# A convolution ahead of a two-layer network: columns 16 to 31 added on VectorE, and the softmax sums of batches 3 to 15 made by accumulating transfers

## The chip, the cores and the metric

The kernel runs on one core of a Trainium2 chip. The metric is the device time of one execution in microseconds (us); before the change the median of three runs is 410.81 us. Below, PE is TensorE, DVE is VectorE, ACT is ScalarE, POOL is GpSimd and SP is SyncE.

## The reference

```
w = exp(weight_gen - max); w = w / sum(w)        # softmax over the K = 7 taps, per position and head
out[b, s, h, g] = sum_k w[b, s, h, k] * x_pad[b, s + k, h, g]      # 8 heads, 192 channels
h1 = out @ w1;  h2 = out @ w2                    # 192 -> 1024
result = maximum(h1, h2) @ w_out                 # 1024 -> 192
```

x is 8 x 4160 x 192, in float32. The 33,280 positions lie on 128 partitions with 260 positions, here called columns, on each.

## The kernel before, in words

**Batches, units, tiles.** The 260 columns are cut into 17 batches: batches 0 to 15 of 16 columns and batch 16 of 4. A batch is cut into units: of 4 columns in batches 0 and 1 (units 0 to 7), of 8 after that. A unit has as many tiles as columns, so tile t has its number in common with a column; a tile holds one eighth (in a 4-column unit, two eighths) of the 1024 hidden values of its unit's columns. Tiles go through PE in groups, of two up to tile 15 and of three from tile 16 (GROUPS, L71).

**Softmax.** For batch b, `load_wg` (L101) brings the taps in, `exp_sum` (L131, ACT) writes their exponentials to `e_t`, `red` (L143, DVE) adds the seven of each head, `ln` (L149, ACT) takes the logarithm of the sums, `shift` (L153, DVE) subtracts it from the taps, and `weights` (L159, ACT) takes the exponential again, which is the normalised weight, written twice in bf16.

**Convolution.** `mul` (L173, DVE) multiplies the seven shifted copies of x by the weights into `m_t`. `adds` (L188, DVE) sums the seven taps in three instructions: taps 3 to 5 onto 0 to 2 (L198), two pairs (L204), and the last pair into `y_t` (L207). Its argument `beside` puts other small DVE steps between the three: a third of `shift` of the next batch, or a half of `red` of a later one. `transpose` (L212) moves `y_t` of a unit through a transposing transfer issued by SP into `yt`. On POOL it then queues a one-element copy (`gate`, L224) that waits for that `yt`, and behind it the loads of x for a later batch and of the taps of batch b + 3.

**The first columns take another way.** `sum_transpose` (L239) sums and transposes on PE: for each of 6 slices and for each tap it multiplies a part of `m_t` by the identity, accumulating in PSUM, and ACT copies the result to `yt` (L255). Units 0 to 4 sum all seven taps so; units 5 to 7 only taps 0, 1, 2 and 6 (`LEFT`), after DVE has done the first of its three additions (`adds(..., first=True)`).

**The two layers.** `hid_tile` (L291, PE) makes a tile's difference of the two products and `relu` (L306, ACT) its positive part; `out_first` and `out_second` (L345, L361, PE) multiply that by w_out (L339) and add the unit's columns times `w10`, the product of w1 and w_out (L351), which gives the results of finished columns, and `evac` (L377, ACT) copies them out of PSUM. `hidden` (L458) puts one group in order: the tiles but one, the first half of the results, relu, the last tile, the second half, the copy out. The results that a group takes (`OUTS`, L426 to L432) are planned from when units are complete, with at most 2 or 4 columns in a group.

**What sets the order.** The order on each engine is the order in which the program writes its instructions; nothing is moved by a scheduler. From group 8 on, `steps` (L768) writes the ACT steps of the softmax at fixed tile numbers (`due`, L721 to L732) and the DVE steps in `extra` (L748): `mul` of the next batch at tile 0 of a batch, its second half at tile 8, and so on. The groups before that have hand-written steps (`early`, L712). Waits are made from the reads and writes of the tiles. POOL issues in order: an instruction that waits holds all behind it.

## Time and profile before

| what | value |
|---|---|
| median of three runs | 410.81 us (410.8 to 415.66) |
| the profiled execution, first to last instruction | 409.1 us |
| PE matmul busy | 398.8 us (97%), 7350 instructions |
| DVE busy | 374.4 us (92%), 219 instructions |
| ACT busy | 357.4 us (87%) |
| POOL busy | 68.7 us (17%) |
| transfers issued by SP, share of the 16 engines | 36.0% |
| transfers issued by POOL, share of the 16 engines | 29.5% |
| granted TensorE clock, mean | 0.997 |

The span is 1.7 us below the median of the runs, which also hold what lies before the first and after the last instruction. Busy shares are means over the whole span; whether an engine's time sets the end must be read from the waits. A busy PE here is nearly one without gaps: matmuls follow each other, and the "idle before" columns name the gaps.

### The profile page before, as it was taken

To read this page: it belongs to the slowest core of one execution; us is meant where nothing else is said; L and a number is where in the kernel's file an instruction comes from. 1 tells how busy PE (TensorE), PEld (TensorE's weight loads), DVE (VectorE), ACT (ScalarE), POOL (GpSimd) and SP (SyncE) were. 2 spreads that over 40 slices of the span, in tenths; PEclk is the share of its full clock that TensorE was granted. 3 is DMA by queue.
4 is the path that set the end of the run, shared out by engine and by line. 5 is a ranking of instruction groups with operands and counts; after the bars stand their busy time and mean duration, and the time that the engine had idled before them with its cause. 6 is when DMAs were issued, how large, how long until landed. Compare 5 with 4: busy or idle time off the path is not lost.

```text
span 409.1 us, 15992 instructions
## 1 busy us (share of the span) xinstructions
PE 398.8 (97%) x7350; PEld 317.1 (78%) x7350; DVE 374.4 (92%) x219; ACT 357.4 (87%) x424; POOL 68.7 (17%) x101
## 2 busy tenths in 40 slices
PE   7999999999999999999999999999999999999995
PEld 2688999677777777777777777777787777787795
DVE  6999999999999999999999999999999999999000
ACT  6899989999999988999988999988999989888771
POOL 0321101222211021221101221210122212210000
PEclk9999999999999999999999999999999999999998
DMA  8966667658657874963796497489648648744513
GB/s 245 250 152 164 116 151 186 143 143 184 150 97 219 217 118 99 260 176 74 224 195 146 96 251 180 82 195 238 120 106 241 166 64 244 151 89 79 213 61 136
DMA packets 60384, 65.68 MB, mean 161 GB/s; under 512 B 47615, under 2 KB 48511, under 8 KB 60318
## 3 DMA queue, kind: packets, MB, share of 16 engines
q1 hardware_dynamic: 51934, 40.54, 36.0%
q0 software_dynamic: 8240, 24.04, 29.5%
q8 instruction: 57, 0.93, 0.9%
q10 hardware_dynamic: 144, 0.10, 0.1%
q14 instruction: 9, 0.07, 0.1%
HBM read 35.96 MB, written 25.56 MB: 150 GB/s over the span
## 4 chain that ended last, share of the span: by engine, by line
DVE 73%; PE 17%; issue 4%; DMA 4%; SPq 0%; DVEq 0%; ACT 0%
DVE m_t L182 37%; DVE m_t L198 15%; DVE m_t L204 10%; PE op_ps L339 9%; PE hd L299 7%; DVE sum_t L147 3%; DVE y_t L207 3%; DVE wg_t L156 3%; DMA xs<-in_x_dram 3%; PE op_ps L351 2%; DMA yt<-y_t 1%; DVE wd L582 0%; DVE xb_t L618 0%; SPq L521 0%; SPq L104 0%
## 5 line engine op out<-in xcount | busy, mean ns | idle before, releaser
L309 ACT ACTIVATE rd_t<-hd 128x1024 bf16<-128x1024 f32 (+1 forms) x206 | 234.6, 1189 | 28.0 <-PE hd L299 26.5
L339 PE MATMUL op_ps<-wo,rd_t 64*128 64x192 bf16 x4160 | 210.6, 243 | 0.1
L339 PEld LDWEIGHTS <-rd_t 64*128 64x128 bf16 x4160 | 180.8, 94 | 15.7 <-ACTq L372 0.3
L299 PE MATMUL hd<-yt,wd 64*128 64x512 bf16 (+1 forms) x1584 | 187.3, 360 | 1.4 <-ACT rd_t L309 1.2
L182 DVE TENSOR_TENSOR m_t<-xb_t,en_t 128x10752 bf16<-128x10752 bf16 (+1 forms) x37 | 187.4, 5071 | 0.2
L299 PEld LDWEIGHTS <-wd 64*128 64x128 bf16 x1776 | 94.1, 94 | 43.3 <-issue 3.3
L224 POOL CAST gate<-yt 128x1 f32<-128x1 bf16 x29 | 34.0, 1171 | 275.7 <-DMA yt<-y_t 275.7
L198 DVE TENSOR_TENSOR m_t<-m_t 128x4608 bf16<-128x4608 bf16 (+1 forms) x32 | 76.8, 2401 | 0.1
L395 ACT COPY o_t<-op_ps 128x384 f32<-128x384 f32 (+1 forms) x99 | 57.3, 591 | 13.4 <-PE op_ps L339 13.3
L351 PE MATMUL op_ps<-w,yt 64*128 64x192 bf16 x780 | 55.5, 243 | 1.1 <-ACT o_t L395 1.0
L351 PEld LDWEIGHTS <-yt 64*128 64x128 bf16 x780 | 38.4, 94 | 17.5 <-issue 2.1
L204 DVE TENSOR_TENSOR m_t<-m_t 128x3072 bf16<-128x3072 bf16 (+1 forms) x29 | 50.0, 1724 | 0.1
L167 ACT ACTIVATE en_t<-wg_t 128x896 bf16<-128x896 f32 (+2 forms) x45 | 35.3, 820 | 0.0
L207 DVE TENSOR_TENSOR y_t<-m_t 128x1536 bf16<-128x1536 bf16 (+1 forms) x29 | 27.3, 941 | 0.5
L385 DVE COPY o_last<-op_ps 128x192 f32<-128x192 f32 x1 | 0.4, 358 | 25.9 <-ACT o_last L385 25.9
L156 DVE TENSOR_TENSOR wg_t<-wg_t,sum_t 128x280 f32<-128x280 f32 (+5 forms) x46 | 22.0, 481 | 0.0
L147 DVE TENSOR_REDUCE sum_t<-e_t 128x64 f32<-128x448 f32 (+2 forms) x31 | 19.6, 636 | 2.6 <-ACT e_t L135 2.6
L114 POOL DMA_DIRECT2D xb_t<-in_x_dram x33 | 17.7, 535 | 23.3 <-ACT rd_t L309 11.8
L135 ACT ACTIVATE e_t<-wg_t 128x896 f32<-128x896 f32 (+2 forms) x18 | 16.1, 899 | 2.5 <-DMA wg_t<-in_weight_gen_dram 2.5
L309 ACT ACTIVATE rd_t<-hdp 128x1024 bf16<-128x1024 f32 x16 | 16.2, 1048 | 0.6 <-PE hdp L299 0.6
L613 PE MATMUL warm<-ident 128*128 128x512 bf16 x38 | 11.0, 457 | 2.6 <-DVE ident L560 2.6
L299 PE MATMUL hdp<-yt,wd 64*128 64x256 bf16 x192 | 12.9, 269 | 0.1
(46 smaller groups left out, 73.6 us busy)
## 6 DMA issues: line engine op xcount, KB each, us to landing
out_dram<-o_t SPq DMA_DIRECT2D x28, 768.0 KB, 5.0
xb_t<-in_x_dram POOLq DMA_DIRECT2D x30, 384.0 KB, 5.2
wg_t<-in_weight_gen_dram POOLq DMA_DIRECT2D x14, 448.0 KB, 5.2
xb_t<-xb_t POOLq DMA_DIRECT2D x16, 288.0 KB, 5.2
out_dram<-o_t SPq DMA_DIRECT2D x8, 384.0 KB, 2.9
wg_t<-in_weight_gen_dram SPq DMA_DIRECT2D x2, 448.0 KB, 4.5
xs<-in_x_dram SPq DMA_DIRECT2D x2, 384.0 KB, 6.0
xb_t<-in_x_dram POOLq DMA_DIRECT2D x3, 192.0 KB, 5.1
```

The source lines that it names most:

```text
L156: nc.vector.tensor_tensor(out=w_t, in0=w_t, in1=_sub(s_ts[b], hs.start, [[1, hs.stop - hs.start], [0, K]]), op=ALU.subtract)
L167: nc.scalar.activation(out=_sub(en_ts[b], (o * WGC + j * N * K) * 2, [[2 * N, K], [2, N], [1, 2]]), in_=_sub(wg_ts[b], (o * H + j * N) * K ...
L182: return nc.vector.tensor_tensor(out=m_out, in0=x_in, in1=_sub(en_ts[b], o * WGC * 2, [[2, K * n * H], [0, G // 2], [1, 2]]), op=ALU.mult,)
L198: nc.vector.tensor_tensor(out=taps(0, 1, 3), in0=taps(0, 1, 3), in1=taps(3, 1, 3), op=ALU.add)
L204: nc.vector.tensor_tensor(out=taps(0, 2, 2), in0=taps(0, 2, 2), in1=taps(1, 5, 2), op=ALU.add)
L207: nc.vector.tensor_tensor(out=_sub(y_ts[b], o * D, [[64, 2], [P, 3 * w // 2], [1, 64]]), in0=taps(0, 1, 1), in1=taps(2, 1, 1), op=ALU.add,)
L224: nc.gpsimd.tensor_copy(out=gate, in_=yt[:, 0:1])
L299: nc.tensor.matmul(hid_out(t, f, j), lhsT=wd_at(j, s, f // 4, f % 4 * P, P), rhs=_sub(yt_ts[u][half(j), :], (s + j) % 3 * P, [[3 * P, w // ...
L309: relu_of[t0] = nc.scalar.activation(out=rd[:, k * 1024:(k + n) * 1024], in_=hd[:, at:at + n * 1024], func=AF.Relu)
L339: return nc.tensor.matmul(op_out(c), lhsT=rd[half(r), k * 1024 + at:k * 1024 + at + P], rhs=wo[half(r), f * D:(f + 1) * D], start=False, s ...
L351: nc.tensor.matmul(op_out(c + j), lhsT=yt_ts[u][half(j), (3 * i + (s + j) % 3) * P:(3 * i + (s + j) % 3 + 1) * P], rhs=w10[half(j), s * D: ...
L395: nc.scalar.copy(out=_sub(o, c % 24 * D, [[D, len(qs)], [h * D, 2], [1, D]]), in_=_sub(tile_, at + (qs[0] - p) * D, [[D, len(qs)], [512, 2 ...
```

## The change

Batch 1 is cut into two units of 8 columns, and is summed by DVE and moved by transposing transfers like the later batches; only batch 0 keeps 4-column units and `sum_transpose`. So `adds` runs in full for both units of batch 1, the steps for units 4 to 7 on PE and their ACT copies are gone, and with `ready` computed from the larger units the plan of results changes in the first groups: group 4 takes no results where it took 2 columns.

For batches 3 to 15 (`by_dma`), `exp_sum` writes `e_t` as seven planes, one for each tap, and `tap_planes` adds them by three accumulating transfers issued by POOL, each reading what the one before it wrote: planes 3 to 5 onto 0 to 2, then planes 2 and 6 onto 0 and 1, then plane 1 onto 0. `red` does nothing for these batches and `ln` reads plane 0. Their `shift` is done in six parts, three beside each `adds`, where it was in three beside the first. The tile numbers of the ACT steps are new, and the taps are loaded half a batch earlier.

```
-        for w in (4, 4, 4, 4) if b < 2 else (8, 8) if n == 16 else (n,):
+        for w in (4, 4, 4, 4) if b == 0 else (8, 8) if n == 16 else (n,):
...
     def exp_sum(b, i=0, of=1):
...
+        if by_dma(b):
+            N = BATCHES[b][1] * H
+            nc.scalar.activation(out=_sub(e_ts[b], 0, [[N, K], [1, N]]), in_=_sub(wg_ts[b], 0, [[1, K], [K, N]]),
+                                 func=AF.Exp)
+            return
...
+    def by_dma(b):
+
+        return 3 <= b < NB - 1
+
+    def tap_planes(b):
+
+        N, e_t = BATCHES[b][1] * H, e_ts[b]
+        for to, frm in (((0, [[1, 3 * N]]), (3 * N, [[1, 3 * N]])),
+                        ((0, [[N, 2], [1, N]]), (2 * N, [[4 * N, 2], [1, N]])),
+                        ((0, [[1, N]]), (N, [[1, N]]))):
+            nc.gpsimd.dma_start(out=_sub(e_t, *to), in_=_sub(e_t, *frm), accum_op=ALU.add)
...
     def ln(b, i=0, of=1):
+        if by_dma(b):
+            N = BATCHES[b][1] * H
+            s_ts[b] = psm.tile([P, N], FP32, name="sum_t", tag="sum")
+            nc.scalar.activation(out=s_ts[b], in_=e_ts[b][:, 0:N], func=AF.Ln)
+            return
...
     def transpose(u):
...
-        if o == 0 and b + 3 < NB:
-            load_wg(b + 3, nc.gpsimd)
+        if u == 4:
+            load_wg(4, nc.gpsimd)
+        if o == 8 and b + 4 < NB:
+            load_wg(b + 4, nc.gpsimd)
...
-        weights(1, 4)
-        mul(1, 4)
         relu(rd, 7, 1)
         exp_sum(2)
-        red(2)
-        adds(1, 4, True)
+        adds(1, 0, beside=lambda i, of: red(2, i, 2) if i < 2 else None)
         sum_transpose(3)
         weights(1, 8)
...
     def end_of_1():
-        shift(2)
-        adds(1, 8, True)
-        mul(1, 12)
+        transpose(4)
         exp_sum(3)
-        red(3)
-        adds(1, 12, True)
+        tap_planes(3)
+        adds(1, 8, beside=lambda i, of: shift(2, i, 2) if i < 2 else None)
...
     early = {
-        3: (none, rest_of_1),
-        4: (lambda: (behind(relu_of[8], load_x(2, 0, 8, halo=False)), sum_transpose(4),
-                     behind(yt_of[4], load_wg(4, nc.gpsimd))), end_of_1),
-        5: (lambda: sum_transpose(5, LEFT), none),
-        6: (lambda: (behind(relu_of[12], load_x(2, 8, 8)), weights(2, 8), ln(3), sum_transpose(6, LEFT)), none),
-        7: (lambda: (behind(relu_of[14], load_x(3, 0, 8)), sum_transpose(7, LEFT)), none),
+        4: (lambda: behind(relu_of[8], load_x(2, 0, 8, halo=False)), lambda: ln(2), end_of_1),
     }
 
     due = {}
-    for c in range(3, NB):
-        soon = c < 8
-        parts_ = [(16 * (c - 2) + (8 if soon else 10 if c < NB - 1 else 15), True, lambda c=c: weights(c, 0))]
-        if 8 in dict(pieces(c)):
-            parts_.append((16 * (c - 2) + (14 if soon else 15), True, lambda c=c: weights(c, 8)))
+    for c in range(2, NB):
+        t0 = 16 * (c - 2)
+        if c == 2:
+            parts_ = [(16, True, lambda: weights(2, 0)), (20, True, lambda: weights(2, 8))]
+        else:
+            parts_ = [(t0 + (11 if c < NB - 1 else 15), True, lambda c=c: weights(c, 0)),
+                      (t0 + 3, False, lambda c=c: ln(c))]
+            if 8 in dict(pieces(c)):
+                parts_.append((t0 + 20, True, lambda c=c: weights(c, 8)))
         if c > 3:
-            ln_at = -2 if c == 4 else 0 if c < 8 else 2 if c < 11 else 4
-            parts_.append((16 * (c - 2) + ln_at, False, lambda c=c: ln(c)))
-            parts_.append((16 * (c - 3) + (4 if c < 8 else 7), True, lambda c=c: exp_sum(c)))
+            parts_.append((t0 - 14, True, lambda c=c: (exp_sum(c), by_dma(c) and tap_planes(c))))
...
-        if s == 8 + later and b + 2 < NB:
-            adds(b + 1, 8, beside=lambda i, of: red(b + 3, i, 2) if b + 3 < NB and i < 2 else None)
-        if k == n // 4 - 1 and 7 < u + 1 < NU:
+        if s == 13 and b + 2 < NB:
+            adds(b + 1, 8, beside=lambda i, of: (shifts(b + 2, 3 + i) if by_dma(b + 2) else None,
+                                                 red(b + 3, i, 2) if b + 3 < NB and i < 2 else None))
+        if k == n // 4 - 1 and u + 1 < NU:
             transpose(u + 1)
+
+    def shifts(c, i):
+
+        if c < NB:
+            shift(c, i, 6 if by_dma(c) else 3)
```

## The prediction

> **What bounds the kernel now.** I read the chain of waits first. It names DVE.
>
> ```profile
> DVE 73%; PE 17%; issue 4%; DMA 4%; SPq 0%; DVEq 0%; ACT 0%
> DVE m_t L182 37%; DVE m_t L198 15%; DVE m_t L204 10%; PE op_ps L339 9%; PE hd L299 7%; DVE sum_t L147 3%; DVE y_t L207 3%; DVE wg_t L156 3%; DMA xs<-in_x_dram 3%; PE op_ps L351 2%; DMA yt<-y_t 1%; DVE wd L582 0%; DVE xb_t L618 0%; SPq L521 0%; SPq L104 0%
> ```
>
> DVE carries it until 328 us, then PE to the end. But a chain follows whatever came last, by however little. So next the timeline where it changes engine (start, duration, engine, line; in brackets the idle time before, and who ended it):
>
> ```profile
> 327.12 0.96 DVE L207 TENSOR_TENSOR y_t<-m_t 128x1536 bf16<-128x1536 bf16 x1
> ...
> 328.23 1.42 SPq L216 DMA_TRANSPOSE yt<-y_t  x1
> ...
> 333.50 0.82 PE L299 MATMUL hd<-yt,wd 64*128 64x512 bf16 x6 [0.20 <-DMA yt<-y_t]
> ...
> 333.58 0.21 POOL L224 CAST gate<-yt 128x1 f32<-128x1 bf16 x1 [10.63 <-DMA yt<-y_t]
> ```
>
> PE waited 0.20 us for this `yt`, its only wait on a transposed unit. Elsewhere the gate copy on POOL marks the landing: unit 8 (tiles from 32) at 61.68, while PE reaches tile 32 at 68.93 (in its timeline 18 matmuls start at 68.27, 12 of them tile 31). The lead is 7.3 us there, 3.9 at tile 96 (155.6 against 159.5), 1.2 at tile 200, 0 at tile 216, and after that about 1 again, as the last batches need fewer small steps. DVE needs 23.67 us per batch (`mul` at 67.66 to `mul` at 91.33), PE 23.09 (tile 72 at 124.95 to tile 208 at 321.21, 8.5 batches). DVE loses to PE slowly and ends level. Both bound the kernel; PE has nearly no gaps, as its busy time by stage shows (from:to, length, then busy us and instructions of PE, PEld, DVE, ACT, POOL):
>
> ```profile
> 30.00:59.60 29.60, 28.60 (x768) 27.93 (x770) 29.60 (x17) 27.95 (x39) 3.22 (x6) 1.00 0.66 148
> 59.60:113.00 53.40, 52.51 (x925) 42.00 (x921) 53.33 (x31) 49.00 (x57) 12.17 (x15) 1.00 0.69 162
> 113.00:333.00 220.00, 219.60 (x3813) 171.09 (x3810) 219.66 (x120) 199.56 (x224) 39.74 (x54) 1.00 0.69 164
> ```
>
> From 113 to 333 PE idles 0.4 us of 220, at full clock. So taking work off DVE brings nothing by itself. What counts is when PE gets going and what it has left.
>
> **PE's own work.** Units 4 to 7 had 84 + 3 x 48 matmuls of `sum_transpose`: 1.23 us at 34.13 and 0.70 each at 38.24, 42.78 and 46.36, 3.3 us in all. The hidden tiles cost the same (a 4-column tile, 12 matmuls, 0.66 us; an 8-column tile, 6 matmuls, 0.66 us). So PE's floor is 409.1 - 3.3 = 405.8, or 407.5 with the 1.7 us around the span. By that alone the kernel can't gain 2%.
>
> **DVE.** Away go 26 reductions: 24 of 64 sums at 0.614 and batch 3's 1.08, 15.8 us. `adds` of batch 1 takes 2 x (2.55 + 1.75 + 0.955) = 10.5 in place of 3 x 1.35: +6.4. `shift` in six parts: rows of 128x112 at 0.269 and 128x280 at 0.443 give 0.327 for 168; so 2 x 0.269 + 4 x 0.327 = 1.85 for 1.39, 0.46 busy, of which 0.08 per extra instruction overlaps its neighbour: +0.23 on the path per batch. Per batch DVE then needs 23.67 - 2 x 0.53 + 0.23 = 22.84, under PE's 23.09. The loss of lead ends.
>
> **The first 60 us, step by step.** DVE reaches `mul(2,0)` later: full `adds` (+6.2 with overlaps), one `mul` less to start (-0.3), no `red(3)` (-1.0), the sums and shift of batch 2 in halves (+0.2): 44.0 becomes about 49.3. On the way `y_t` of unit 4 ends at 37.5; the first transfer took 5.7 from there (55.9 to 61.68), so `yt` lands at 43.2, just when PE wants tile 16 (43.5, below). The second ends at 49.4.
>
> Group 4 gives PE no results now. Counting `OUTS` by its formula, 16 columns have results when tile 25 starts, where 20 had; the four are made good only by group 18. Two columns cost 0.25 + 1.32 = 1.57 us (6 matmuls of L351, 32 of L339), so PE carries 3.1 us of its work past tile 25.
>
> ACT: relu 9 ends at 34.0, `ln(2)` waits for the sums on DVE until 35.0, then `exp_sum(3)` (0.9) and relus of 0.95 follow: relu 15 ends at 43.4, so PE starts tile 16 at 43.5 (47.43 before). Relus 16 to 18 and the copy end at 48.3, `weights(2,0)` at 49.3, `exp_sum(4)` at 50.8 (its taps land about 49.9), relus 19 to 21 and the copy at 54.0. Then comes `ln(3)`. PE, with hidden PSUM for three tiles, idles meanwhile: tile 19 waits until 47.0, tile 22 until 52.7.
>
> **The sums by transfers.** `tap_planes(3)` is three transfers, each issued after the landing of the one before, all on POOL. POOL's queue ahead of them: the gate for unit 4 (43.3, up to 1.8 us long in the rows), a load of x, a load of taps (0.53 and 0.55); so the first goes out at about 45.0. Behind POOL's waits stand `tap_planes(4)`, the gate of unit 5 and the x of batch 3, due for `mul(3,0)` at 74 and here by 68: covered by 6 us.
>
> No row shows an accumulating transfer. The nearest is the copy within SBUF, `xb_t<-xb_t`, 288 KB: alone in the queue at 30.06 it landed in 2.5 us; the median, queued behind a load of x, is 5.2:
>
> ```profile
> xb_t<-xb_t POOLq DMA_DIRECT2D x16, 288.0 KB, 5.2
> ```
>
> is the page's row of the whole span (number of issues, size, median from issue to landing), and from 28 to 34 us the only one is
>
> ```profile
> xb_t<-xb_t POOLq DMA_DIRECT2D x1, 288.0 KB, 2.5
> ```
>
> The first link stands behind two loads: 5.2, landing at 50.3. The others stand alone and are smaller, but read their destination too: between 2.5 and 5.2, I take 3.0 each. A link below 2.5 isn't excluded for 64 and 128 KB; at 1.8 the wait is gone. Sum: 50.3 + 6.0 = 56.3, against ACT's arrival at 54.0. ACT stands 2.4 us with relu 22 behind `ln(3)`; PE waits for that relu, and DVE with `shift(3)`, done with `mul(2,0)` at 55.1, waits too. Then `ln` 0.3, `weights(2,8)` 1.05, relus 22 and 23 1.9: PE starts tile 25 at 59.7. Before it was 59.6.
>
> The Trainium skill's page "DMA: Bandwidth & Descriptors", section "Rules for kernel authors", speaks against this tree of sums: a transfer that reads what another wrote must wait for that one's completion. Its section "Anatomy of one DMA — SWDGE (gpsimd) path" fits a fixed 2.0 us plus bytes at 436 GB/s, an estimate of 2.3 and 2.2 for the last two links; by it the sums would be there at 54.8 and the span 1.5 us shorter. For the 288 KB of the lone copy the fit gives 2.7 where the trace has 2.5; for an accumulating one no row here shows it.
>
> **The sum.** Before, PE went from tile 25 at 59.6 to the end at 409.1. Now: 59.7 + 349.5 + 3.1 = 412.3, less the 0.2 waited at 333.5: 412.1. Later starvation I cost at nothing, since the units lead: `adds(2,0)` runs from 56.8 to 62.6 and its `yt` lands at 66.6, PE takes tile 32 at 69.0; tile 40's lands at 78.0, wanted at 81.4; and then DVE is the faster. If that cover were gone, the late transfers (5.4 against a median of 3.9) would cost up to 1.5. Later sums have room: from `exp_sum(c)` to `ln(c)` are 17 tiles, 24.5 us, against 5.2 + 6.0; for batches 5, 8, 11 and 14, whose transfers are written after a gate, some 3 us remain at links of 4.5. ACT loses four copies of 0.82, under cover. With 1.7 around the span: **414 us**, 0.7% slower, within 2%.
>
> **The rivals.** First, no wait at `ln(3)`: links of 1.8, or the first not behind the loads (45.0 + 3 x 2.5 = 52.5). Then relu 22 starts 2.4 earlier: 409.7, 411.4 with the rest; were the other early gaps (tiles 19 and 22) smaller too, down to the floor of 407.5. For it: the transfers are small. Against: POOL's queue holds two loads just ahead.
>
> Second, slower: the links cost 5.2 and more. At 5.2 `ln(3)` runs at 60.7, and the time is 418.2; from 5.7 on it is over 419.0, the 2% bound. At 7.0 it is 422, and the transfers of batches 5, 8, 11 and 14, which start only behind a gate, come 2 us late four times: 430. For it: 15 of the 16 copies in the trace took over 4 us, the transfer engines are 69% busy, and two of the three move runs of 512 bytes, where the copy moves 2304. Against: those copies stood behind a load.
>
> Third, faster by over 2%: the chain is to be taken at its word and DVE sets the end. Then the 11 batches of sums before 328 us are worth 11 x 1.06 - 11 x 0.23 - 5.3 = 3.8 us: 407. Even that isn't 2%; it needs a PE gap that no view shows.
>
> **How the numbers follow.** `ln(3)` holds ACT by a few us: 0.52, 411 to 418. No wait: 0.24. Slow links: 0.20. Faster by over 2%: 0.04 (2% is about what a measurement here tells from no change). So within 2% has 0.76. The range runs from 407, the floor, to 423, links of about 7 without the repeats.
>
> **What would show it.** ACT's wait on a transfer of `e_t` at `ln` of batch 3, near 54 us, and no other; tile 25 near 59.7 us, and a lead of the units over PE that stays at 2 to 4 us afterwards; PE without gaps from 60 us on; no reductions after batch 3. I am wrong if PE idles after 113 us, if tile 25 starts after 62, or if a link is over 5.7 us.

## The result, and the profile after

The changed kernel takes 461.36 us, median of 4 runs (453.76 to 471.82), against 411.36 before (four runs, one more than in the table above): ratio 1.1062, 95% interval 1.0944 to 1.1179. It is 11% slower, where the prediction had 414 us. The profiled execution took 464.18 us with a span of 462.3; it is one of the two longer ones, and the ratio is formed from the other two (453.76 and 458.53).

The page's chain of work that ended last, by engine and by line, no longer reads like two engines without gaps:

```profile
PE 36%; DMA 20%; issue 19%; DVE 9%; POOL 9%; ACT 5%; POOLq 0%; ACTq 0%; SPq 0%; DVEq 0%
PE op_ps L361 15%; PE hd L321 14%; DMA e_t<-e_t 11%; DMA xb_t<-in_x_dram 6%; DVE m_t L206 5%; POOL e_t L152 3%; POOL gate L246 3%; ACT rd_t L331 3%; DMA yt<-y_t 3%; PE op_ps L373 3%; PE warm L635 2%; DVE m_t L222 2%; DMA xb_t<-xb_t 1%; DVE m_t L226 1%; ACT en_t L191 1%
```

DVE had 73% of that chain. Now it has 9%, and in its place stand transfers (the links of the sums, loads of x, the transposing transfer) and two instructions of POOL: the issue of the links (L152) and the gate copy (L246). POOL, 17% busy before, is on the path.

The busy time by stage (from:to, length, then busy us and instructions of PE, PEld, DVE, ACT, POOL, then granted clock, share of the transfer engines, GB/s) shows where PE, which had 0.4 us idle in 220, now stands:

```profile
60.00:113.00 53.00, 50.74 (x816) 38.64 (x817) 49.36 (x33) 45.70 (x50) 27.46 (x19) 0.94 0.72 157
113.00:220.00 107.00, 89.93 (x1550) 69.26 (x1547) 84.47 (x50) 81.55 (x88) 44.79 (x35) 0.97 0.76 153
220.00:290.00 70.00, 57.68 (x896) 43.08 (x897) 53.43 (x36) 52.17 (x55) 28.00 (x22) 0.90 0.75 149
```

From 113 to 290 us every engine has gaps, DVE included (84.5 of 107 us where it was full). POOL's busy time has more than doubled, over the span from 68.7 to 165.5 us; that of PE and ACT grew by 8 and 9 us, that of DVE fell by 4. PE's ledger closes: it is busy 407.1 us, 8.3 more than before, though it has 324 matmuls fewer (228 of `sum_transpose`, worth the 3.3 us, and 96 since an 8-column tile takes 6 where a 4-column one takes 12); and it idles 55.2 us where it idled 10.3. Together that is the 53.2 us by which the span grew.

Tile by tile, PE starts tile 24 at 56.1 us, 1.5 earlier than before, tile 32 3.9 later, tile 104 14.2 later, tile 152 43.2 later and tile 200 51.6 later; from there to the end the gap stays at 52. So the loss is not one event at the start: most of it, 29 us, falls between tiles 104 and 152.

The view of waits (engine, line, what it waited for: us in total, times, longest) names the new ones:

```profile
POOL e_t L152 <- DMA e_t<-e_t: 121.8, 25, 9.9
...
DVE m_t L206 <- DMA xb_t<-in_x_dram: 19.8, 4, 5.1
PE hd L321 <- DMA yt<-y_t: 19.5, 6, 10.5
...
DVE wg_t L180 <- ACT sum_t L172: 15.7, 8, 6.0
ACT sum_t L172 <- DMA e_t<-e_t: 13.2, 4, 4.2
DVE m_t L206 <- DMA xb_t<-xb_t: 13.2, 3, 10.1
```

POOL stands 121.8 us before the issue of a link, for the landing of the one before it. Read from the bottom: DVE waits for the halo (the columns that a batch shares with the one before it, copied from that one's x: `xb_t<-xb_t`) and for x (13.2 + 19.8 us), ACT for the sums and DVE for ACT's logarithm behind them (13.2, 15.7), PE for a transposed unit (19.5). None of these was in the trace before, but for PE's one wait of 0.2 us. All of those loads and links are issued by POOL, in order.

**The start went as predicted.** The timeline (start, duration, engine, line; in brackets the idle time before and who ended it) of POOL, and ACT at `ln` of batch 3:

```profile
41.83 1.71 POOL L246 CAST gate<-yt 128x1 f32<-128x1 bf16 x1 [6.98 <-DMA yt<-y_t]
43.49 0.54 POOL L114 DMA_DIRECT2D xb_t<-in_x_dram  x1
44.01 0.55 POOL L104 DMA_DIRECT2D wg_t<-in_weight_gen_dram  x1
44.55 0.93 POOL L152 DMA_DIRECT2D e_t<-e_t  x1
51.04 1.23 POOL L152 DMA_DIRECT2D e_t<-e_t  x1 [5.56 <-DMA e_t<-e_t]
55.11 1.78 POOL L152 DMA_DIRECT2D e_t<-e_t  x2 [2.85 <-DMA e_t<-e_t]
...
57.59 0.31 ACT L172 ACTIVATE sum_t<-e_t 128x128 f32<-128x128 f32 x1 [2.41 <-DMA e_t<-e_t]
```

The links take 6.2, 3.8 and 2.4 us and ACT waits 2.41. PE starts tile 25 at 60.7, against 59.7 forecast. The trouble lies in the rest of the picture: from 44.6 to 57.5 us POOL does nothing but this chain and the issue of the next chain's first link, and later it does much worse. The gate copies, as one row of the tile's view (duration in ns: least, median, most):

```profile
L246 POOL CAST gate<-yt x31: 185/1077/13936, 41.8 to 436.3; 128x1 f32<-128x1 bf16 x31
```

Before, the row read:

```profile
L224 POOL CAST gate<-yt x29: 183/1557/1868, 61.7 to 384.4; 128x1 f32<-128x1 bf16 x29
```

One element per partition took at most 1.87 us and now takes up to 13.9. What one such copy stands beside is in the timeline of POOL and, below it, of DVE:

```profile
94.18 9.90 POOL L246 CAST gate<-yt 128x1 f32<-128x1 bf16 x1
104.03 0.56 POOL L114 DMA_DIRECT2D xb_t<-in_x_dram  x1
...
95.26 0.33 DVE L180 TENSOR_TENSOR wg_t<-wg_t,sum_t 128x168 f32<-128x168 f32 x1
95.50 1.76 DVE L226 TENSOR_TENSOR m_t<-m_t 128x3072 bf16<-128x3072 bf16 x1
...
97.42 0.96 DVE L229 TENSOR_TENSOR y_t<-m_t 128x1536 bf16<-128x1536 bf16 x1
98.28 5.75 DVE L206 TENSOR_TENSOR m_t<-xb_t,en_t 128x10752 bf16<-128x10752 bf16 x1
106.46 0.28 DVE L180 TENSOR_TENSOR wg_t<-wg_t,sum_t 128x112 f32<-128x112 f32 x1 [2.42 <-ACT sum_t L172]
```

The copy ends at 104.08, when `mul` has ended and DVE has nothing to start for 2.42 us. Until then it is passed over by five instructions of DVE in a row, all with two inputs and each starting about 0.08 us before the one ahead of it ends. Before, 27 of the 29 copies ended with the first instruction of DVE that they met, 26 times a `mul`; the other two took 0.18 us, one beside a reduction and one beside nothing. Two things on DVE are new here: the one-input reductions are gone, and a short part of `shift` (L180, 0.27 to 0.33 us) stands in every slot between the large instructions.

### The profile page after: what moved, and what is told of

It is laid out like the page before. It is cut to its first block, busy times and chain, and to the rows that moved or that the text cites. A ratio compares the mean times of both kernels' runs of the same rounds, so it can differ in the third digit from the quotient of the medians.

```text
span 462.3 us, 15418 instructions
## 1 busy us (share of the span) xinstructions
PE 407.1 (88%) x7026; PEld 313.1 (68%) x7026; DVE 370.6 (80%) x236; ACT 366.8 (79%) x412; POOL 165.5 (36%) x142
## 4 chain that ended last, share of the span: by engine, by line
PE 36%; DMA 20%; issue 19%; DVE 9%; POOL 9%; ACT 5%; POOLq 0%; ACTq 0%; SPq 0%; DVEq 0%
PE op_ps L361 15%; PE hd L321 14%; DMA e_t<-e_t 11%; DMA xb_t<-in_x_dram 6%; DVE m_t L206 5%; POOL e_t L152 3%; POOL gate L246 3%; ACT rd_t L331 3%; DMA yt<-y_t 3%; PE op_ps L373 3%; PE warm L635 2%; DVE m_t L222 2%; DMA xb_t<-xb_t 1%; DVE m_t L226 1%; ACT en_t L191 1%
## 5 line engine op out<-in xcount | busy, mean ns | idle before, releaser
L361 PE MATMUL op_ps<-wo,rd_t 64*128 64x192 bf16 x4160 | 214.1, 245 | 9.1 <-ACTq L394 9.0
L206 DVE TENSOR_TENSOR m_t<-xb_t,en_t 128x10752 bf16<-128x10752 bf16 (+1 forms) x35 | 187.4, 5355 | 41.3 <-DMA xb_t<-in_x_dram 19.8
L321 PE MATMUL hd<-yt,wd 64*128 64x512 bf16 (+1 forms) x1488 | 191.0, 379 | 28.1 <-DMA yt<-y_t 19.5
L321 PEld LDWEIGHTS <-wd 64*128 64x128 bf16 x1680 | 89.3, 95 | 78.5 <-issue 36.6
L246 POOL CAST gate<-yt 128x1 f32<-128x1 bf16 x31 | 96.5, 3113 | 95.0 <-DMA yt<-y_t 95.0
L152 POOL DMA_DIRECT2D e_t<-e_t x39 | 39.8, 1029 | 134.2 <-DMA e_t<-e_t 121.8
L180 DVE TENSOR_TENSOR wg_t<-wg_t,sum_t 128x168 f32<-128x168 f32 (+4 forms) x86 | 28.2, 329 | 15.7 <-ACT sum_t L172 15.7
L136 ACT ACTIVATE e_t<-wg_t 128x896 f32<-128x896 f32 x13 | 24.2, 1864 | 13.0 <-DMA wg_t<-in_weight_gen_dram 12.8
L114 POOL DMA_DIRECT2D xb_t<-in_x_dram x33 | 24.3, 737 | 15.1 <-DVE m_t L206 10.4
L127 POOL DMA_DIRECT2D xb_t<-xb_t x16 | 14.6, 910 | 16.7 <-DMA xb_t<-in_x_dram 16.7
L104 POOL DMA_DIRECT2D wg_t<-in_weight_gen_dram x15 | 14.1, 937 | 9.3 <-ACT rd_t L331 5.4
```

Of the source, the lines that this page charges most:

```text
L152: nc.gpsimd.dma_start(out=_sub(e_t, *to), in_=_sub(e_t, *frm), accum_op=ALU.add)
L206: return nc.vector.tensor_tensor(out=m_out, in0=x_in, in1=_sub(en_ts[b], o * WGC * 2, [[2, K * n * H], [0, G // 2], [1, 2]]), op=ALU.mult,)
L246: nc.gpsimd.tensor_copy(out=gate, in_=yt[:, 0:1])
L321: nc.tensor.matmul(hid_out(t, f, j), lhsT=wd_at(j, s, f // 4, f % 4 * P, P), rhs=_sub(yt_ts[u][half(j), :], (s + j) % 3 * P, [[3 * P, w // ...
L361: return nc.tensor.matmul(op_out(c), lhsT=rd[half(r), k * 1024 + at:k * 1024 + at + P], rhs=wo[half(r), f * D:(f + 1) * D], start=False, s ...
```

## The experiments

What was open: which of the change's parts costs the 50 us. Four theories at first. A: the chained links hold POOL's queue by their waits. B: the gate copies are held up by VectorE. C: the new way of columns 16 to 31 costs it. D: loads that leave late run beside transposing transfers and stretch them. What holds the copies became a question of its own, taken up from e12 on.

**e1, one part alone: columns 16 to 31.** All sums stay on VectorE.

```
     def by_dma(b):
-        return 3 <= b < NB - 1
+        return False
...
-        tap_planes(3)
         adds(1, 8, beside=lambda i, of: shift(2, i, 2) if i < 2 else None)
+        red(3)
```

> The changed kernel with the sums of batches 3 to 15 on VectorE again, so that only the new way of columns 16 to 31 is left. Two theories name the accumulating transfers and their queue as the cause (A: their waits hold POOL, and with it the loads of x and of the taps; B: with VectorE's reductions gone, the gate copies on POOL find no break between VectorE's instructions). Both expect nearly all of the loss gone here: VectorE starts batch 2 some 5 us later than before and keeps its 23.67 us per batch, so 416 us, between 411 and 422. Theory C, that the new way of columns 16 to 31 upsets the start and what follows from it, expects over 440 us.

417.59 us, ratio 1.0149 (1.0127 to 1.0172). That is 6 us of the 50; theory C falls. DVE is busy 106.83 of the 107 us from 113 to 220 and PE follows it: each unit but the last lands 0 to 2 us before PE wants it. The longest copy takes 2.82 us:

```profile
L246 POOL CAST gate<-yt x31: 184/1717/2822, 42.5 to 391.5; 128x1 f32<-128x1 bf16 x31
```

**e2 and e2b, the other part alone.** The kernel before, with sums by transfers for batches 4 to 15, ACT's steps at the changed kernel's tile numbers. In e2 the old tile numbers of the weights were kept, so that for some batches the second half of the weights is taken ahead of its shift; e2b has the order right.

```
+    def by_dma(b):
+        return 4 <= b < NB - 1
...
-            parts_.append((16 * (c - 2) + ln_at, False, lambda c=c: ln(c)))
+            parts_.append((16 * (c - 2) + 3, False, lambda c=c: ln(c)))
+            parts_.append((max(16, 16 * (c - 3) + 2), True, lambda c=c: (exp_sum(c), by_dma(c) and tap_planes(c))))
```

> The kernel before with only the sums of batches 4 to 15 moved to accumulating transfers, with the tile numbers for exponential, logarithm, shift and loads of taps as in the changed kernel; columns 16 to 31 go as before. Theories A and B expect the loss here: 440 to 470 us. Theory C expects 408 to 418 us.

> The kernel before with only the sums of batches 4 to 15 moved to accumulating transfers, with the tile numbers of exponential, logarithm, shift, both halves of the weights and the loads of taps as in the changed kernel, so that the weights follow the shift (in the run before this one their second half could come ahead of it). The transfers on POOL are the cause: 440 to 475 us. They do harm only together with the new way of columns 16 to 31: 408 to 420 us.

e2: 477.68 us, 1.1605 (1.1527 to 1.1683). e2b: 459.89 us, 1.1164 (1.1075 to 1.1254). This part, which holds the transfers and the `shift` in six parts, loses what the whole change loses, without batch 1's new way and without batch 3's chain at the start. The gate copies stretch to 17.7 us here too, and POOL waits 113.7 us for links. The cause is in this part; A, B or both.

**e3, no gate copy.** The loads wait for the transposing transfer themselves.

```
-        nc.sync.dma_start_transpose(
+        moved = nc.sync.dma_start_transpose(
...
-        nc.gpsimd.tensor_copy(out=gate, in_=yt[:, 0:1])
...
-            load_x(c, 0, min(8, BATCHES[c][1]))
+            behind(moved, load_x(c, 0, min(8, BATCHES[c][1])))
```

> The changed kernel without the gate copy on POOL: the loads behind it wait for the transposing transfer itself. The order of the loads is the same, but no POOL instruction has to read SBUF beside VectorE. Theory B expects at least half of the loss back: under 438 us, and POOL's busy time down by some 96 us. Theory A expects 445 to 465 us, since the waits for the accumulating transfers stay.

436.41 us, 1.0584 (1.0544 to 1.0624): 20 of the 50 us were the copies. POOL's busy time falls from 165.5 to 76.4 us. What stays is partly in one place, unit 6. The timeline of POOL there, and the busy time in steps of 4 us:

```profile
62.70 0.90 POOL L152 DMA_DIRECT2D e_t<-e_t  x1 [2.26 <-DMA e_t<-e_t]
63.27 0.90 POOL L114 DMA_DIRECT2D xb_t<-in_x_dram  x1
63.81 0.94 POOL L127 DMA_DIRECT2D xb_t<-xb_t  x1
64.36 0.94 POOL L104 DMA_DIRECT2D wg_t<-in_weight_gen_dram  x1
80.46 0.54 POOL L114 DMA_DIRECT2D xb_t<-in_x_dram  x1 [15.16 <-DMA yt<-y_t]
```

```profile
72.00:76.00 4.00, 0.00 (x0) 0.00 (x0) 4.00 (x4) 0.00 (x0) 0.00 (x0) 0.60 0.81 84
76.00:80.00 4.00, 0.00 (x0) 0.00 (x0) 4.00 (x1) 0.00 (x0) 0.00 (x0) 0.50 1.25 48
```

The chain released three loads at once, at 63.3 to 64.4, when the transfer of unit 6 had just been issued (63.51). It landed at 80.18, 16.7 us later; the transfer engines are busy (shares of 0.81 and 1.25) and move 84 and 48 GB/s. PE idles about ten us, and its clock has halved meanwhile.

**e4, the links apart.** Links 2 and 3 are written later in the program, so that POOL needn't wait between them.

```
-            parts_.append((t0 - 14, True, lambda c=c: (exp_sum(c), by_dma(c) and tap_planes(c))))
+            parts_.append((t0 - 14, True, lambda c=c: (exp_sum(c), by_dma(c) and tap_planes(c, (0,)))))
+            if by_dma(c):
+                parts_.append((t0 - 6, False, lambda c=c: tap_planes(c, (1,))))
+                parts_.append((t0 - 2, False, lambda c=c: tap_planes(c, (2,))))
```

> The changed kernel with the three accumulating transfers of a batch (from batch 4) put apart in POOL's queue: the first where it was, the second 8 tiles and the third 12 tiles later, each behind the gate and the loads that were due in between. Theory A expects most of the loss back: under 430 us, the 121.8 us of POOL's waits for these transfers down to under 50. Theory B expects 445 to 465 us, gate copies as long as in the changed kernel.

463.77 us, 1.1264 (1.1236 to 1.1292): nothing gained, the interval even lies above that of the changed kernel, and A's expectation failed. The reason is in POOL's timeline, and in two rows of the waits:

```profile
69.58 12.00 POOL L248 CAST gate<-yt 128x1 f32<-128x1 bf16 x1 [7.94 <-DMA yt<-y_t]
...
82.10 0.92 POOL L154 DMA_DIRECT2D e_t<-e_t  x1
```

```profile
DVE wg_t L182 <- ACT sum_t L174: 43.0, 12, 5.5
...
ACT sum_t L174 <- DMA e_t<-e_t: 32.2, 5, 7.7
```

The later links now stand behind a gate copy, of 12.0 us here, so the sums come late for ACT, and DVE waits for ACT. A was neither refuted nor shown by this: it can be seen only with the copies gone.

**e5, both.** The edits of e3 and e4 together:

```
-        nc.gpsimd.tensor_copy(out=gate, in_=yt[:, 0:1])
...
+                parts_.append((t0 - 6, False, lambda c=c: tap_planes(c, (1,))))
+                parts_.append((t0 - 2, False, lambda c=c: tap_planes(c, (2,))))
```

> The changed kernel with both earlier edits: no gate copy on POOL, and the second and third accumulating transfer of a batch 8 and 12 tiles after the first. If the gate copies held the later links in the run with links apart (12 us at units 6, 12, 18 and 24, then ACT waits at the logarithm), and the waits between the links hold the loads in the run without copies, then the two together give most of both back: 414 to 426 us. If the accumulating transfers cost by their traffic instead, it stays at 434 to 445 us.

427.59 us, 1.0375 (1.034 to 1.0409), a little above the range. Against e3 the links apart are worth 9 us, so A and B are both true, and B hides A. The 9 us aren't the whole price of the links' waits: POOL still waits 84.6 us for links here, against 105.1 in e3. The transposing transfers land in 3.6 to 6.4 us, and each unit lands at least 1.5 us before PE wants it. 16 us remain against the kernel before: 6.4 of them are there by tile 40.

**e6, the loads let go in the kernel before.** Its copy and the wait in it are dropped, so its loads run beside the transposing transfers.

```
-        nc.gpsimd.tensor_copy(out=gate, in_=yt[:, 0:1])
```

> The kernel before without the gate copy and without its wait: the loads of x and taps go as soon as their buffers are free, so beside the transposing transfers. Theory D, that loads beside a transposing transfer stretch it (the stalls of 10 to 16 us from issue to landing in the changed kernel), expects transposes that take over 8 us from issue to landing and a time over 425 us. If the stretched transposes come from the accumulating transfers alone, they stay under 6 us and the time at 409 to 414 us.

412.55 us, 1.0016 (1.0002 to 1.0031). The transfers' longest time to landing grows from 5.4 to 7.8 us, not further, and the units' lead covers it. So D at this price is false: a load beside a transposing transfer stretches it by a few us, and the kernel before has room for that. The 10 to 17 us of the changed kernel were seen where several loads and links stood beside one transfer; how many it takes wasn't tried.

**e7, a gate that reads nothing.** In place of the copy, POOL waits for the transfer and writes a constant.

```
-        nc.gpsimd.tensor_copy(out=gate, in_=yt[:, 0:1])
+        behind(moved, nc.gpsimd.memset(gate, 0.0))
```

> The changed kernel with the gate copy replaced by a POOL instruction that only writes one element and waits for the same transposing transfer. If it is the read of SBUF that finds no break beside VectorE's two-input instructions, the gates take under 0.5 us each and the time is that of the run without the copy, 432 to 442 us. If any POOL instruction on SBUF has to wait so, it stays at 450 to 470 us.

442.83 us, 1.0773 (1.0731 to 1.0815), just above what was expected, and the gates:

```profile
L246 POOL MEMSET gate<- x31: 93/99/488, 41.3 to 412.2; 128x1 f32 x31
```

Same place in the queue, same wait, same size: 99 ns in the median and 0.49 us at most, where the copy took 1077 and 13.9 us. It is the read that is held up, not the place in the queue. Why this kernel is still 6 us behind e3 (8 by the ratios) is open; PE waits 15.3 us for transposed units here and 10.8 there.

**e8, the exponential's read in order.** ACT's exponential into planes (L136) takes 1.87 us where the same 896 elements took about 1 before. Here, on top of e5, the read runs in order and the write steps.

```
-            nc.scalar.activation(out=_sub(e_ts[b], 0, [[N, K], [1, N]]), in_=_sub(wg_ts[b], 0, [[1, K], [K, N]]),
+            nc.scalar.activation(out=_sub(e_ts[b], 0, [[1, N], [N, K]]), in_=_sub(wg_ts[b], 0, [[K, N], [1, K]]),
```

> The run without copies and with links apart, its exponential into planes now reading the taps in order and writing with a step of one plane, where it read with a step of seven and wrote in order; the same values land in the same places. In the changed kernel these 13 instructions took 1.86 us, against 0.98 for the same number of elements before. If the stepped read is what costs, they take about 1.0 us here and the time falls to 415 to 422 us; if the stepped write costs as much, they stay at 1.8 us or more, and the time at 425 to 430 us.

425.08 us, 1.0318 (1.0246 to 1.0391). The second branch of the expectation holds: the thirteen exponentials take 1.81 us in the median. The stepped write costs about as much here as the stepped read.

**e9, the exponential in halves,** written three tiles apart, on top of e5.

```
+            M = N // of
+            nc.scalar.activation(out=_sub(e_ts[b], i * M, [[N, K], [1, M]]),
+                                 in_=_sub(wg_ts[b], i * M * K, [[1, K], [K, M]]), func=AF.Exp)
...
+                parts_.append((t0 - 14, True, lambda c=c: exp_sum(c, 0, 2)))
+                parts_.append((t0 - 11, True, lambda c=c: (exp_sum(c, 1, 2), tap_planes(c, (0,)))))
```

> The run without copies and with links apart, with the exponential into planes cut into two instructions of half the heads, three tiles (one group) apart. If what is left of the loss is ACT's steps that meet in one group of results (exponential, logarithm and weights, 3.1 us in a row, while PE waits up to 1.5 us for the copy behind them), the time falls to 417 to 424 us though ACT has no less to do. If ACT's sum of work or the traffic of the transfers is the limit, it stays at 425 to 430 us.

426.23 us, 1.0344 (1.0296 to 1.0392), in the range of the rival, and the interval overlaps that of e5: nothing shown by itself. A half takes 1.05 us, and PE's wait for ACT's copies of results falls from 6.1 to 3.3 us.

**e10, batch 3 back on VectorE,** on top of e5.

```
-        return 3 <= b < NB - 1
+        return 4 <= b < NB - 1
...
-        tap_planes(3)
         adds(1, 8, beside=lambda i, of: shift(2, i, 2) if i < 2 else None)
+        red(3)
```

> The kernel without the gate copy and with the links of the sums written apart (427.59 us), but with batch 3's sums back on VectorE: transfers make the sums of batches 4 to 15 only, so ScalarE no longer meets the first chain at ln of batch 3, near 54 us. Theory: what that kernel loses beyond the price of batch 1's new way (some 10 us) is lost mostly at the start, where it is 6.4 us behind the kernel before by tile 40. Then tile 40 starts within 1 us of the kernel before, TensorE keeps its clock there, and the time is 419 to 422 us. Rival: the loss is spread, from the long exponentials on ScalarE; then the units are late elsewhere and the time is 425 us or more.

421.96 us, 1.0254 (1.0232 to 1.0276), as the theory had it: tile 40 starts 0.3 us after that of the kernel before, where e5 was 6.4 late. Only the clock isn't kept throughout: there is one stretch of 3.4 us at half clock, from 53.9 us. The first chain and what follows it are worth 5 us. PE's waits from 100 to 330 us are all for ACT:

```profile
PE op_ps L374 <- ACT o_t L418: 4.6, 3, 1.5
PE hd L322 <- ACT rd_t L332: 1.9, 3, 0.7
```

**e11, e10 with the exponentials in halves,** by the lines of e9:

```
+                parts_.append((t0 - 14, True, lambda c=c: exp_sum(c, 0, 2)))
+                parts_.append((t0 - 11, True, lambda c=c: (exp_sum(c, 1, 2), tap_planes(c, (0,)))))
```

> The kernel with batch 3's sums on VectorE (421.96 us) and, on top, the exponential of batches 4 to 15 written in two halves three tiles apart. Between 100 and 330 us TensorE waited there 4.6 us for ScalarE's copies of results behind the whole exponential, and 1.9 us for relus. Theory: the long exponential on ScalarE is what is left; with halves the copies' wait falls to about 2.6 us and the time to 419 to 421 us. Rival: what is left lies in gaps of TensorE too short to be named as waits; then the waits shrink and the time stays at 421.5 to 423 us.

418.2 us, 1.016 (1.0123 to 1.0196). The interval lies below that of e10; the gain, some 4 us, is larger than the theory's. The wait for copies falls from 4.6 to 2.1 us.

So the loss can be laid out by steps of ratio times 411 us: the gate copies 20 us (1.1062 to 1.0584), the waits between links 9 (to 1.0375), the first chain 5 (to 1.0254), the long exponentials 4 (to 1.016), and 6.6 that stay. The intervals leave the first step at 15 to 25 us and the others at about 2 us either way. These are steps in this order; e4 shows that another order would give other shares, and the halves alone, worth 4 us here, gave 1.3 on top of e5, within its noise. What stays is about the size of e1's 1.5%, but the limit isn't the same: in e1 DVE is full, in e11 it has gaps (103.7 of 107 us from 113 to 220). That rest wasn't split. No version comes below the kernel before.

**e12 and e13: what holds the copies?** Two answers were at hand: the reductions are gone from DVE, or the links on POOL, just ahead of the copies, do it. e12 puts idle reductions back in the old places; e13 leaves the transfers out, so that the sums of batches 3 to 15 aren't made.

```
     def red(b, i=0, of=1):
         if by_dma(b):
+            hs, at, ap = part(b, i, of)
+            nc.vector.reduce_sum(out=spare[:, hs], in_=_sub(ones, at, ap), axis=AX.X)
             return
```

```
     def tap_planes(b):
 
         N, e_t = BATCHES[b][1] * H, e_ts[b]
-        for to, frm in (((0, [[1, 3 * N]]), (3 * N, [[1, 3 * N]])),
-                        ((0, [[N, 2], [1, N]]), (2 * N, [[4 * N, 2], [1, N]])),
-                        ((0, [[1, N]]), (N, [[1, N]]))):
-            nc.gpsimd.dma_start(out=_sub(e_t, *to), in_=_sub(e_t, *frm), accum_op=ALU.add)
```

> The changed kernel with VectorE's reductions put back in their old places for batches 4 to 15, but of a constant tile into a spare one, so that nothing waits for them; the sums still come from the transfers. It tells apart what holds the gate copies. If it is the lack of one-input instructions on VectorE: the copies last at most 3 us again, POOL is held some 60 us less, and the time falls to 430 to 450 us, though VectorE has 1.2 us more per batch. If it is the links (a copy that comes upon a transfer's issue or beside an accumulating transfer is passed over until VectorE idles): copies of 8 us and more remain, and the time is 455 us or more.

> The changed kernel with the accumulating transfers left out: the logarithm reads the first plane as it is, so the sum over the taps isn't made for batches 3 to 15 and the output is another. VectorE has no reductions for these batches, POOL no links. If the lack of one-input instructions on VectorE holds the copies, copies of 8 us and more remain here too, and the time stays above 425 us. If the links do, every copy ends at the end of the first VectorE instruction (at most 3 us, as in the kernel before), and the time is 412 to 424 us.

e12: 479.94 us, 1.1558 (1.1487 to 1.1629), copies up to 12.8 us: it isn't the missing reductions alone. e13: 470.64 us, 1.1417 (1.1358 to 1.1475), copies up to 18.9 us: it isn't the links. Both answers failed. Without any link the copies are held longest, several passed over by 13 instructions; DVE waits for sums only 5.7 us here (15.7 in the changed kernel), and it is DVE's waits that let a held copy go: all eight copies over 10 us end when DVE waits for x or its halo. And with reductions back on DVE copies are still held.

**e14 and e15: the parts of `shift`.** What is left is its cut into six parts. e14 goes back to three in the changed kernel; e15 takes e1 and puts six in.

```
         if c < NB and i < 3:
-            shift(c, i, 6 if by_dma(c) else 3)
+            shift(c, i, 3)
```

```
-            shift(c, i, 6 if by_dma(c) else 3)
+            shift(c, i, 6 if 3 <= c < NB - 1 else 3)
```

> The changed kernel with the shift of batches 3 to 15 in three parts beside the first additions of a batch, as in the kernel before, in place of six parts beside both; the sums still come from the transfers. In the traces with held copies a short subtraction (0.27 to 0.33 us) starts 0.08 us before every large VectorE instruction ends, so VectorE never has a gap; with three parts, each second unit's additions follow each other directly and leave 0.03 us between them. Theory: the small steps in every slot hold the copies; then no copy is over 5 us and the time falls to 430 to 448 us. Rival: the missing reductions hold them, or something else; then copies of 8 us and more remain and the time is 450 us or more.

> The kernel with all sums on VectorE (417.59 us) and the shift of batches 3 to 15 in six parts beside both additions, as in the changed kernel: no transfers of sums, reductions in their old places. By the theory of the small steps, copies of 8 us and more appear and the time rises above 440 us. By the rivals (links, missing reductions) copies stay under 3 us and the time is 418 to 422 us, for the longer path on VectorE.

e14: 439.33 us, 1.0692 (1.0641 to 1.0743). The longest copy is 5.9 us, just over the 5 expected, and all but two end with the first instruction they meet. e15: 435.03 us, 1.056 (1.051 to 1.0609), less than the 440 expected, but 17 us more than e1, with copies of up to 13.3 us, and that without one transfer of sums. So the six parts hold the copies, at a price of 15 us in the changed kernel (10 to 20 by the intervals) and of 17 in e1. How, the timeline of e15 shows, POOL's row first, then DVE's:

```profile
78.33 13.33 POOL L246 CAST gate<-yt 128x1 f32<-128x1 bf16 x1 [9.94 <-DMA yt<-y_t]
...
79.99 0.27 DVE L180 TENSOR_TENSOR wg_t<-wg_t,sum_t 128x112 f32<-128x112 f32 x1
80.18 2.55 DVE L222 TENSOR_TENSOR m_t<-m_t 128x4608 bf16<-128x4608 bf16 x1
...
91.34 0.27 DVE L180 TENSOR_TENSOR wg_t<-wg_t,sum_t 128x112 f32<-128x112 f32 x1
91.53 0.61 DVE L166 TENSOR_REDUCE sum_t<-e_t 128x64 f32<-128x448 f32 x1
```

At 79.99 `mul` is followed by a subtraction of 0.27 us, and the copy is passed over; in e1 the same copy meets a subtraction of 0.44 us (three parts) or a reduction there, and ends. Here it ends at 91.66, with the first reduction that it meets. So a reduction does let it through here, but there are two to a batch, beside one unit of two. In e12 two copies that met an idle reduction weren't let through by it (3.1 and 3.2 us). Why the subtraction of 0.44 us lets a copy pass and that of 0.27 mostly doesn't is open.

## Why the prediction was wrong, point by point

**What held.** The first sixty microseconds: the first transfer, 43.2 forecast, landed at 41.8; the first link was forecast to land at 50.3 and landed at 50.75; the sums 56.3 against 57.5; ACT's wait 2.4 against 2.41; tile 25 59.7 against 60.7. The order of magnitude of the links was right as well (5.2, 3.0, 3.0 against 6.2, 3.8, 2.4 in the first chain; medians of 6.5 and 3.8 for the first two over the span).

Relieving DVE brought nothing in these runs: e1 with its full DVE and e11 with a relieved one end within a microsecond of each other. It isn't a clean test, since e11 also carries what its transfers cost. One count of the prediction is off without effect: the reductions that go are 25, not 26, and 15.8 us is the sum of 25.

**The step that failed is "Later starvation I cost at nothing, since the units lead".** The lead of the units was worked out from DVE's and PE's rates alone. It depends on POOL being in time with x, halo and taps, and three costs on POOL were left out of it or priced too low.

1. *"`shift` in six parts: ... +0.23 on the path per batch", and the gate copy "up to 1.8 us long in the rows".* Each was taken by itself. The short parts cost DVE what I said, but they hold the copies on POOL up to 13.9 us: e14 and e15 put 15 and 17 us on the six parts alone, e3 20 us on the copies altogether. The rows for a warning were there: 27 of the 29 copies before ended with an instruction of DVE, which suggests that DVE decides its length. I used its longest duration as if it were a property of the copy.

2. *"Covered by 6 us" and "later sums have room".* I checked that each sum would be ready for ACT: 17 tiles against 11.2 us. I didn't check what else stood in the queue while POOL waited between the links. POOL waits 121.8 us for links, 25 times, and each time the gates and loads of coming units stand behind it. Already the x of batch 3, "here by 68", landed at 74.4 and its halo at 75.1: its gate copy, whose unit had landed at 54.3, came up at 63.55 behind two chains and then took 5.84 us. Part of the waits' price is the 9 us between e3 and e5. The ready time of a result and the hold of the queue that issues it are two sums, and only the first was made.

3. *"The late transfers would cost up to 1.5"* at 5.4 us each. The price was taken from transfers that nothing disturbed. Loads that are released late go out together, beside a transposing transfer, and it lands after up to 15.6 us. The changed kernel's timeline at unit 14:

```profile
149.25 11.81 POOL L246 CAST gate<-yt 128x1 f32<-128x1 bf16 x1
...
161.01 0.56 POOL L114 DMA_DIRECT2D xb_t<-in_x_dram  x1
...
161.17 1.48 SPq L238 DMA_TRANSPOSE yt<-y_t  x1
...
161.68 0.57 POOL L114 DMA_DIRECT2D xb_t<-in_x_dram  x1
...
165.98 5.76 DVE L206 TENSOR_TENSOR m_t<-xb_t,en_t 128x10752 bf16<-128x10752 bf16 x1 [4.96 <-DMA xb_t<-in_x_dram]
...
171.04 0.82 PE L321 MATMUL hd<-yt,wd 64*128 64x512 bf16 x6 [1.12 <-DMA yt<-y_t]
```

A copy of 11.8 us holds two loads of x back until the next unit's transfer starts; all three run together, and the unit lands at 171.0. That PE waits only 1.1 us here is because it had fallen behind already. This is how the three costs feed each other: a late load delays `mul`, a waiting DVE delays the next unit, and a unit that is late meets the loads of the one after it. The hold even ends by its own damage: the copy keeps back the x that `mul` needs next, DVE runs out of work, and only then does the copy get through. The four waits of DVE for x, 19.8 us in all, follow the four copies of 10.5 to 13.9 us in just this way. e6 puts a bound to it: in the kernel before, without the first two costs and without links, letting the loads go is worth 0.2%.

**ACT's exponential was costed at nothing.** "ACT loses four copies of 0.82, under cover" counted what is taken from ACT and not what the plane form adds, 0.9 us on each of thirteen exponentials. In the timeline the long one stands ahead of `ln`, the weights, a relu and the copy that PE waits for:

```profile
79.16 1.87 ACT L136 ACTIVATE e_t<-wg_t 128x896 f32<-128x896 f32 x1
80.91 0.31 ACT L172 ACTIVATE sum_t<-e_t 128x128 f32<-128x128 f32 x1
...
82.92 0.81 ACT L417 COPY o_t<-op_ps 128x768 f32<-128x768 f32 x1
...
83.79 0.42 PE L373 MATMUL op_ps<-w,yt 64*128 64x192 bf16 x6 [1.55 <-ACT o_t L417]
```

PE waits 1.55 us, at full clock, for an ACT that is not idle meanwhile. From e10 to e11, which only cuts the exponential in halves, the time falls by 4 us.

**Right in the mechanism, short in size: what the first chain does.** The forecast of 414 holds one wait of 2.4 us at `ln(3)`. e10 gives the chain 5 us, for behind the wait PE idles and then runs at half its clock (see below), and tile 32 starts at 72.8 where I had 69.0.

**The rivals.** The slower one, slow links, had the right sign and named the right queue, but its price came from ACT waiting for sums (a link over 5.7 us at the start, four late chains later: 430). The first link was 6.2, above its point of decision, yet tile 25 was only 1.0 later than forecast; and ACT's waits for sums, 13.2 us in all, are a small part of the loss. Its mechanism was a result that is late. What happened is a queue that is held. No wait at `ln(3)` fell with the 2.41 us waited there, and nothing bears out DVE's chain at its word: in e11 DVE is relieved and nothing is gained, though the transfers' own price lies in that run too.

## What to carry to other kernels

Before work is moved from a full engine onto a queue that issues transfers, list everything which that queue issues behind each new wait, with its due time: the engine that was relieved waits for those loads next. A duration that an engine shows beside a neighbour belongs to the pair: when the change cuts, adds or removes the neighbour's instructions, look at which of them ended it before, and don't carry the row over. And a synchronising instruction should touch no shared resource: have the loads wait for the event itself, as e3 does.

## What the runs showed of the hardware

**A read on POOL can be held up through many VectorE instructions.** The one-element copy took up to 18.9 us (e13), the write-only gate at most 0.49 (e7). The Trainium skill's page "SBUF — State Buffer", section "Who interferes with whom", says that a VectorE instruction with two SBUF inputs contends with a GpSimd instruction that reads SBUF and not with one that only writes, and that a reduction never does; e7, and the copy that ends with e15's reduction, agree, the two copies of e12 that a reduction didn't let through don't. Of blocking for a whole instruction the section speaks only for VectorE's modes that take two ports. Here, beside instructions with two inputs, the block lasted over 5 to 13 of them that follow each other, and by e14 and e15 it was the short ones in every slot that made it so.

**TensorE's clock halves after it idles.** From 56 to 60 us PE is busy 1.80 of 4 us; then (columns as in the busy time by stage above):

```profile
60.00:62.00 2.00, 1.31 (x8) 0.56 (x9) 2.00 (x3) 1.92 (x3) 0.70 (x1) 0.50 0.45 51
62.00:64.00 2.00, 2.00 (x19) 1.25 (x16) 2.00 (x4) 0.53 (x1) 1.03 (x3) 0.50 0.66 211
...
66.00:68.00 2.00, 2.00 (x34) 1.68 (x32) 2.00 (x1) 1.00 (x2) 2.00 (x4) 0.83 0.73 135
```

The granted clock is 0.50 until about 66.7. The span has 27.2 us of such stretches, 3.4, 6.8, 6.8 and 10.2 us long, worth an estimated 13.6 us at most (half of them); e1 has none and e4 some 41. The Trainium skill's page "TensorE: Matmul & The Clock Gate", in Part 1, has the clock drop to half after an idle window of about 3.4 us and come back after a busy one; the stretches, multiples of 3.4, agree. But the window needn't be idle throughout: in the 3.4 us before the four drops PE was still busy 1.38, 0.53, 0.00 and 1.23 us. Each wait of PE long enough to meet that costs more than itself.

**Transposing transfers stretch beside loads.** Time to landing 3.6 to 5.4 us before, up to 7.8 with single loads let go (e6), up to 16.7 (e3) and 17.2 (e7) with several loads beside one.

**The stepped exponential of the planes costs double on ACT,** whether the step is in the read (1.87 us) or in the write (1.81), for 128x896 float32 that take about 1 us in order. `weights` also steps in its read, but takes each element twice and writes bf16, and needs 1.05 us for 896.
